# Moving tiles in SBUF: v's tiles and the small ones ahead of the activations' parts, T's second buffer behind its first

## The chip, the core and the metric

The kernel runs on one core of a Trainium2 chip. The metric is the device time of one execution in microseconds (us): 853.65 us before, the median of 3 runs (851.96 to 855.98).

## What is computed

Linear attention over 8 batches, 8 heads, 576 tokens and head size 64, then a feed-forward layer over the 4608 tokens with 512 inputs, 2048 hidden units and 512 outputs:

```python
q_s = softmax(q, axis=-1); k_s = softmax(k, axis=2)     # over the features; over the tokens
kv  = einsum('bhsd,bhse->bhde', k_s, v)
x   = einsum('bhsd,bhde->bhse', q_s, kv)                 # then 4608 x 512
h   = x @ w_in
out = (h * sigmoid(1.702 * h)) @ w_out
```

q, k and v are float32, the two weights are float64.

## The kernel before, in words

**Stages.** The 4608 tokens go in nine blocks t of 512 (TB). For each block the attention part makes x, transposed, in four tiles; the feed-forward part then makes eight steps, each with two of the sixteen groups of 128 hidden units (`pair(t, step)` says which two: ascending in even blocks, descending in odd ones).

**Precision by parts.** Each operand of the feed-forward matmuls is split into a high part and a low part, both float32r; a product is three matmuls (high by high, high by low, low by high) into the same PSUM bank.

**First product of a step.** In blocks 0 and 1 it is `plain1` (line 794): per group and 128 inputs three matmuls with 128x128 weights from wj and 512 columns of xp. In blocks 2 to 8 it is `ffn1` (line 841): a two-by-two product made by seven products instead of eight (a Strassen scheme) over halves of 256 tokens. Each of the seven is six matmuls with 128x128 weights and 256 columns. Four of the seven (products 6, 7, 5, 4 in the code) take their weights from T, sums of weight blocks that block 1 computes once and keeps in DRAM; three (1, 2, 3) take them from wj. The streamed operand is always xo. T has two buffers, `wt(0)` and `wt(1)`, here T0 and T1: a step uses buffer `pair % 2`, so in blocks 2 to 8 (56 steps) 28 steps take T0 and 28 take T1. wj has two buffers likewise (wj0x and wj1x).

**Second product.** `ffn2` (line 904) makes, one step later, eight units (four banks by two groups), each of three matmuls with 128x128 weights from the activations' parts (gh, the high one, and gl, the low one) and 512 streamed columns of w, the parts of w_out: 24 matmuls per step, 72 steps. gh and gl have two buffers, used by `step % 2`: gh0/gl0 and gh1/gl1. So in line 904 the activations are the stationary operand and the weights are streamed; in lines 794 and 841 it is the other way about.

In TensorE's queue the units of the second product lie between the products of the next step. A program at build time (`Plan`) sets the order of all instructions from costs and due times; it looks at no address. The attention work of the next block (lines 582 to 587, 634, 683, 704) lies between the steps as well.

**Where tiles lie.** `sb` makes a tile in one pool with one buffer per tag. Tiles are laid one behind the other in the order in which their tags are first asked for, without holes here; the bytes per partition of a tile are the product of its shape without the first number, times 4. Almost all tiles are a multiple of 512 bytes. The exceptions, which shift all that comes behind them: each of the four vt (2 x 4 x 65 x 4 = 2080 bytes, 32 over a multiple of 512), vl (8 x 65 x 4 = 2080, 32 over), the two qm and r (32 each), and `first` (64). Counted from ident, modulo 512, this gives in the kernel before:

| tile | place modulo 512 |
|---|---|
| gh0, gh1, gl0, gl1 | 0 |
| wj, T0 (in the place of `wide`) | 256 |
| T1 (asked for at its first use, behind w and x tiles) | 320 |
| w, xp, xo | 320 |

Slices inside these tiles start at multiples of 512 bytes, so the distance of a matmul's streamed operand from its stationary one, modulo 512, is 64 for wj and T0 (lines 794 and 841), 0 for T1 (line 841), and 320 for the second product (line 904).

Of the kernel before, what the change touches and what calls it, by code (L numbers as in the profile page):

```python
# [10 lines left out]
F32R = mybir.dt.float32r  # L11
# [125 lines left out]
def efficient_attention_then_gelu_ffn(  # L137
# [28 lines left out]
    B, H, S, D = q.shape  # L166
    NTOK, DM = out.shape
    FF = w_out.shape[0]
    P = 128
    C = 4  # L170
    TB = P * C
    HT = TB // 2
    NB = NTOK // TB
    NP = H // 2
# [4 lines left out]
    CM = SM // P  # L179
    ST = S - SM  # L180
    W = D + 1
# [11 lines left out]
    def sb(name, shape, dtype=F32, tag=None):  # L193
        return const.tile(shape, dtype, name=name, tag=tag or name)

    ident = sb("ident", [P, P])
    kvn = [sb(f"kvn{i}", [P, NP, D]) for i in range(2)]
    gt = [[sb(f"g{i}{u}", [P, 2, HT]) for i in range(2 - u)] for u in range(2)]
    gs = [[sb(f"g{s}{i}", [P, 2, 2, HT], F32R) for i in range(2)] for s in "hl"]
    tt = sb("tt", [P, 4, HT])  # L200
    tmp = [sb(f"tmp{i}", [P, DM]) for i in range(2)]
    kt = [sb(f"kt{i}", [P, 2, CM, D]) for i in range(NP)]
    vt = [sb(f"vt{i}", [P, 2, CM, W]) for i in range(NP)]
    qt = [sb(f"qt{i}", [P, C, 2, D]) for i in range(NP)]
    qT = [sb(f"qT{i}", [P, TB]) for i in range(2)]
    mx = [sb(f"mx{i}", [P, 2, D]) for i in range(NP)]
    m1 = sb("m1", [P, 2, 2, D])
    qm = [sb(f"qm{i}", [P, 2 * C]) for i in range(2)]
    r_ = sb("r", [P, 2, NP])
    rs = [r_[:, i] for i in range(2)]  # L210
    kl, vl = sb("kl", [P, H, D]), sb("vl", [P, H, W])
    wj = [[sb(f"wj{i}{jj}", [P, 2, KC, P], F32R) for jj in range(2)] for i in range(2)]
    wts = {}

    def wt(i):
        if i not in wts:
            wts[i] = sb(f"wt{i}", [P, 2, 4, 2 * P], F32R, tag=f"wt{i}")
        return wts[i]


    wide = sb("wide", [P, 4, DM], tag="wt0")
    kept = [[dram.tile([P, 2 * DM], F32, name=f"kept{p}{jj}") for jj in range(2)] for p in range(NS)]
    kept_t = [dram.tile([P, 4 * DM], F32, name=f"kept_t{p}") for p in range(NS)]

# [779 lines left out]
```

## Time and profile before

| | |
|---|---|
| median of 3 runs | 853.65 us |
| the profiled execution, its own time | 853.69 us |
| its span, first to last instruction | 851.9 us |
| TensorE busy | 843.5 us |
| VectorE, ScalarE, GpSimd busy | 525.6, 487.2, 114.3 us |

The span is 1.8 us shorter than the time of that execution: what lies around the first and last instruction. In the profile PE is TensorE with its matmuls, PEld its weight loads, which overlap the matmuls. Matmuls are pipelined, so the duration of one in a row is longer than the distance from its start to the start of the next; times of a stretch are taken from starts. L841 is line 841 of the kernel. Names like `bank<-xo,wt` are output, then inputs, without buffer numbers: T0 and T1 are both "wt", and are told apart by the time at which they run.

### The profile page before, as it was taken

To read this page: it belongs to the slowest core of one execution; us is meant where nothing else is said; L and a number is where in the kernel's file an instruction comes from. 1 tells how busy PE (TensorE), PEld (TensorE's weight loads), DVE (VectorE), ACT (ScalarE), POOL (GpSimd) and SP (SyncE) were. 2 spreads that over 40 slices of the span, in tenths; PEclk is the share of its full clock that TensorE was granted. 3 is DMA by queue.
4 is the path that set the end of the run, shared out by engine and by line. 5 is a ranking of instruction groups with operands and counts; after the bars stand their busy time and mean duration, and the time that the engine had idled before them with its cause. 6 is when DMAs were issued, how large, how long until landed. Compare 5 with 4: busy or idle time off the path is not lost.

```text
span 851.9 us, 14617 instructions
## 1 busy us (share of the span) xinstructions
PE 843.5 (99%) x5643; PEld 722.3 (85%) x5644; DVE 525.6 (62%) x1082; ACT 487.2 (57%) x833; POOL 114.3 (13%) x175
## 2 busy tenths in 40 slices
PE   9999999999999999999999999999999999999998
PEld 4687787778888898888888998899888899889986
DVE  8899896999627875467554765375356533453333
ACT  5799769768537758465744675464356433343322
POOL 1000020120113011111211121100110011101110
PEclk9999999999999999999999999999999999999999
DMA  9999935893479467564845665623654165416541
GB/s 290 283 339 359 265 132 187 263 320 133 129 233 239 129 161 223 173 186 100 246 158 163 165 184 171 177 88 116 204 162 138 50 198 174 148 50 198 173 148 50
DMA packets 127845, 155.63 MB, mean 183 GB/s; under 512 B 76576, under 2 KB 105760, under 8 KB 121376
## 3 DMA queue, kind: packets, MB, share of 16 engines
q0 software_dynamic: 25248, 83.37, 31.7%
q1 hardware_dynamic: 102528, 71.32, 28.2%
q8 instruction: 45, 0.74, 0.4%
q14 instruction: 24, 0.20, 0.1%
HBM read 128.45 MB, written 26.21 MB: 182 GB/s over the span
## 4 chain that ended last, share of the span: by engine, by line
PE 87%; DVE 6%; DMA 4%; ACT 1%; issue 1%; POOL 0%; SPq 0%; DVEq 0%; ACTq 0%; POOLq 0%
PE bank L904 42%; PE bank L841 33%; PE bank L794 5%; DMA raw<-in_moe_w_out 3%; PE bank L634 2%; PE bank L704 2%; PE bank L683 2%; PE bank L296 1%; DVE w L368 1%; DVE gl L812 1%; DVE wide L333 1%; DVE raw L337 0%; PE bank L582 0%; PE bank L583 0%; DMA vt<-in_v 0%
## 5 line engine op out<-in xcount | busy, mean ns | idle before, releaser
L904 PE MATMUL bank<-w,gh 128*128 128x512 f32 x1152 | 361.0, 395 | 0.0
L904 PE MATMUL bank<-w,gl 128*128 128x512 f32 x576 | 226.3, 393 | 0.4 <-DVE gl L812 0.4
L904 PEld LDWEIGHTS bank<-w,gh 128*128 128x128 f32 x1152 | 192.7, 188 | 25.0 <-issue 2.7
L841 PEld LDWEIGHTS bank<-xo,wt 128*128 128x128 f32 x1344 | 187.8, 188 | 17.8
L841 PE MATMUL bank<-xo,wt 128*128 128x256 f32 x1344 | 193.8, 281 | 0.0
L841 PE MATMUL bank<-xo,wj 128*128 128x256 f32 x1008 | 146.2, 280 | 0.5 <-ACT tt L865 0.5
L841 PEld LDWEIGHTS bank<-xo,wj 128*128 128x128 f32 x1008 | 136.3, 188 | 12.1 <-issue 1.6
L854 DVE TENSOR_TENSOR g<-bank,tt 128x256 f32<-128x256 f32 x168 | 71.0, 423 | 102.9 <-PE bank L841 101.3
L904 PEld LDWEIGHTS bank<-w,gl 128*128 128x128 f32 x576 | 108.3, 188 | 24.9 <-DVE gl L812 0.9
L857 ACT ACTIVATE g<-g 128x512 f32<-128x512 f32 x112 | 58.8, 525 | 121.8 <-DVE g L854 118.8
L854 DVE TENSOR_TENSOR tt<-bank,tt 128x256 f32<-128x256 f32 x112 | 47.3, 423 | 130.3 <-PE bank L841 96.3
L397 POOL DMA_DIRECT2D wj<-kept x96 | 59.4, 619 | 364.1 <-PE bank L841 307.0
L794 PE MATMUL bank<-xp,wj 128*128 128x512 f32 x384 | 103.8, 396 | 1.2 <-ACT g L809 0.9
L885 DVE TENSOR_TENSOR gl<-g,gh 128x512 fp32r<-128x512 f32 x112 | 77.3, 691 | 23.3 <-ACT gh L882 22.7
L794 PEld LDWEIGHTS bank<-xp,wj 128*128 128x128 f32 x384 | 71.2, 188 | 19.6 <-ACT g L809 1.3
L882 ACT CAST gh<-g 128x512 fp32r<-128x512 f32 x112 | 69.5, 621 | 3.5
L545 POOL PARTITION_ALL_REDUCE mx<-mx x32 | 32.3, 1009 | 192.9 <-DVE mx L541 167.4
L857 ACT ACTIVATE g<-bank 128x256 f32<-128x256 f32 x56 | 21.6, 386 | 53.3 <-PE bank L841 52.5
L865 ACT COPY tt<-bank 128x256 f32<-128x256 f32 x56 | 20.8, 372 | 50.6 <-PE bank L841 50.3
L397 POOL DMA_DIRECT2D wt<-kept_t x42 | 22.2, 530 | 148.8 <-PE bank L841 148.8
L687 ACT COPY qT<-bank 128x512 f32<-128x512 f32 x36 | 20.5, 588 | 22.3 <-PE bank L683 21.9
L664 ACT ACT_TABLE_LOAD x25 | 32.1, 1283 | 0.4
(103 smaller groups left out, 802.4 us busy)
## 6 DMA issues: line engine op xcount, KB each, us to landing
wt<-kept_t POOLq DMA_DIRECT2D x42, 1024.0 KB, 5.2
wj<-kept POOLq DMA_DIRECT2D x54, 512.0 KB, 3.7
wj<-kept POOLq DMA_DIRECT2D x42, 256.0 KB, 4.9
out<-tmp SPq DMA_DIRECT2D x36, 256.0 KB, 2.8
kt<-in_k SPq DMA_DIRECT2D x32, 256.0 KB, 4.1
raw<-in_moe_w_in SPq DMA_DIRECT2D x16, 512.0 KB, 8.4
raw<-in_moe_w_out SPq DMA_DIRECT2D x16, 512.0 KB, 7.1
kept<-wj SPq DMA_DIRECT2D x16, 512.0 KB, 6.8
```

The source lines that it names most:

```text
L397: "POOL", 1.0, (key,), (ring,), R(t, step - 2, off), lambda: nc.gpsimd.dma_start(out=out(), in_=src), size=size
L545: nc.gpsimd.partition_all_reduce(flat, flat, P, bass_isa.ReduceOp.max)
L664: nc.scalar.activation(x, x, AF.Exp)
L687: plan.add("ACT", act(TB), (PB,), (Q,), rank, lambda: nc.scalar.copy(qT[hp % 2], pq))
L794: nc.tensor.matmul(bank[bk], w[:, l, c, :], x[:, r], start=c == 0 and e == 0, stop=c == KC - 1 and e == 2)
L841: nc.tensor.matmul(ph[bk], w, x[:, r, c, :], start=opens and c == 0 and e == 0, stop=c == 1 and e == 2, skip_group_check=True,)
L854: return lambda: nc.vector.tensor_tensor(out=o, in0=ph[bk], in1=x, op=ALU.add)
L857: return lambda: nc.scalar.activation(o, x, AF.Gelu_apprx_sigmoid)
L865: vec("ACT", act(n), (ZB,), (A,), 2, lambda: nc.scalar.copy(a, ph[Z]))
L882: vec("ACT", act(2 * n), half, H, slot, lambda c=c, gh=gh: nc.scalar.copy(gh, c))
L885: nc.vector.tensor_tensor(out=gl, in0=c, in1=gh.bitcast(F32), op=ALU.subtract)
L904: nc.tensor.matmul(bank[c], l, r, start=first_ and e == 0, stop=last and e == 2)
```

## The change

Only the order in which the tiles are asked for is changed. vl, qm and r come first, ahead of ident; the second buffers of gh and gl come behind vt, which comes behind their first buffers; T1 is asked for right behind `wide` (T0's place). No instruction, no size and no plan entry changes.

```diff
+    vl = sb("vl", [P, H, W])
+    qm = [sb(f"qm{i}", [P, 2 * C]) for i in range(2)]
+    r_ = sb("r", [P, 2, NP])
+    rs = [r_[:, i] for i in range(2)]
     ident = sb("ident", [P, P])
     kvn = [sb(f"kvn{i}", [P, NP, D]) for i in range(2)]
     gt = [[sb(f"g{i}{u}", [P, 2, HT]) for i in range(2 - u)] for u in range(2)]
-    gs = [[sb(f"g{s}{i}", [P, 2, 2, HT], F32R) for i in range(2)] for s in "hl"]
+    gs = [[sb(f"g{s}0", [P, 2, 2, HT], F32R)] for s in "hl"]
+    vt = [sb(f"vt{i}", [P, 2, CM, W]) for i in range(NP)]
+    for s, g in zip("hl", gs):
+        g.append(sb(f"g{s}1", [P, 2, 2, HT], F32R))
     tt = sb("tt", [P, 4, HT])
     tmp = [sb(f"tmp{i}", [P, DM]) for i in range(2)]
     kt = [sb(f"kt{i}", [P, 2, CM, D]) for i in range(NP)]
-    vt = [sb(f"vt{i}", [P, 2, CM, W]) for i in range(NP)]
...
-    qm = [sb(f"qm{i}", [P, 2 * C]) for i in range(2)]
-    r_ = sb("r", [P, 2, NP])
-    rs = [r_[:, i] for i in range(2)]
-    kl, vl = sb("kl", [P, H, D]), sb("vl", [P, H, W])
+    kl = sb("kl", [P, H, D])
     wj = [[sb(f"wj{i}{jj}", [P, 2, KC, P], F32R) for jj in range(2)] for i in range(2)]
-    wts = {}
+
+    wide = sb("wide", [P, 4, DM], tag="wt0")
+    wts = {1: sb("wt1", [P, 2, 4, 2 * P], F32R)}
...
-    wide = sb("wide", [P, 4, DM], tag="wt0")
```

Counted from the first tile, modulo 512, vl, qm and r take 32 + 64 + 32 = 128, so gh0 and gl0 lie at 128; the four vt add 128, so gh1, gl1, wj, T0 and T1 lie at 256; `first` adds 64, so w, xp and xo lie at 320. The distance, streamed minus stationary, becomes:

| matmuls | before | after |
|---|---|---|
| L794 and L841 with wj, L841 with T0 | 64 | 64 |
| L841 with T1 (28 steps x 24) | 0 | 64 |
| L904 with gh0, gl0 (864) | 320 | 192 |
| L904 with gh1, gl1 (864) | 320 | 64 |

## The prediction

> **What bounds the kernel.** I read first the page with its busy shares and the chain that ended last, then the groups of instructions, then the timeline of TensorE step by step.
>
> ```profile
> span 851.9 us, 14617 instructions
> ...
> PE 843.5 (99%) x5643; PEld 722.3 (85%) x5644; DVE 525.6 (62%) x1082; ACT 487.2 (57%) x833; POOL 114.3 (13%) x175
> ...
> PE 87%; DVE 6%; DMA 4%; ACT 1%; issue 1%; POOL 0%; SPq 0%; DVEq 0%; ACTq 0%; POOLq 0%
> ...
> L904 PE MATMUL bank<-w,gh 128*128 128x512 f32 x1152 | 361.0, 395 | 0.0
> ...
> L841 PE MATMUL bank<-xo,wt 128*128 128x256 f32 x1344 | 193.8, 281 | 0.0
> ...
> L841 PE MATMUL bank<-xo,wj 128*128 128x256 f32 x1008 | 146.2, 280 | 0.5 <-ACT tt L865 0.5
> ```
>
> TensorE is busy for 99% of the span and is 87% of the chain, and the two feed-forward lines have no idle time worth naming before their matmuls (0.0 to 0.5 us per group). So what counts is how fast TensorE goes through a fixed row of matmuls. No instruction changes; time can only come from the distance between starts of neighbouring matmuls, if that depends on where operands lie. Whether it does, the trace of before can show, because its T0 and T1 steps run the same instructions with distances of 64 and 0.
>
> From 768.9 us on, six steps follow each other with no attention work between them. These timeline rows are the first product with T in each step (start, duration, line, operands); the last row is the start of the step behind:
>
> ```profile
> 768.92 0.86 PE L841 MATMUL bank<-xo,wt 128*128 128x256 f32 x6
> ...
> 779.39 0.87 PE L841 MATMUL bank<-xo,wt 128*128 128x256 f32 x6
> ...
> 789.83 0.88 PE L841 MATMUL bank<-xo,wt 128*128 128x256 f32 x6
> ...
> 800.25 0.84 PE L841 MATMUL bank<-xo,wt 128*128 128x256 f32 x6
> ...
> 810.50 0.88 PE L841 MATMUL bank<-xo,wt 128*128 128x256 f32 x6
> ...
> 821.03 0.87 PE L841 MATMUL bank<-xo,wt 128*128 128x256 f32 x6
> ...
> 831.56 0.86 PE L841 MATMUL bank<-xo,wt 128*128 128x256 f32 x6
> ```
>
> Pairs run upward in even blocks, downward in odd ones, and by that the steps from 768.92, 789.83 and 810.50 use T1, those from 779.39, 800.25 and 821.03 use T0. T1 steps last 10.47, 10.42 and 10.53 us, mean 10.473; T0 steps 10.44, 10.25 and 10.53, mean 10.407; all six 62.64 / 6 = 10.44. The view by tile gives the matmuls with T in each of these six steps, in the same order (minimum, median and maximum duration in ns):
>
> ```profile
> L841 PE MATMUL bank<-xo,wt x24: 274/282/287, 768.9 to 776.5; 128*128 128x256 f32 x24
> ...
> L841 PE MATMUL bank<-xo,wt x24: 279/279/281, 779.4 to 786.9; 128*128 128x256 f32 x24
> ...
> L841 PE MATMUL bank<-xo,wt x24: 277/282/287, 789.8 to 797.4; 128*128 128x256 f32 x24
> ...
> L841 PE MATMUL bank<-xo,wt x24: 276/276/276, 800.2 to 807.6; 128*128 128x256 f32 x24
> ...
> L841 PE MATMUL bank<-xo,wt x24: 278/282/287, 810.5 to 818.1; 128*128 128x256 f32 x24
> ...
> L841 PE MATMUL bank<-xo,wt x24: 279/280/283, 821.0 to 828.6; 128*128 128x256 f32 x24
> ```
>
> Each T1 step has matmuls from 274 or 278 up to 287 ns with a median of 282. Each T0 step is nearly uniform, but at 279, 276 or 280. The view by source line gives the second product's matmuls with gh in the three T0 steps:
>
> ```profile
> L904 PE MATMUL bank<-w,gh x16: 392/393/394, 780.8 to 789.4; 128*128 128x512 f32 x16
> ...
> L904 PE MATMUL bank<-w,gh x16: 388/390/392, 801.6 to 810.0; 128*128 128x512 f32 x16
> ...
> L904 PE MATMUL bank<-w,gh x16: 388/397/397, 822.4 to 831.1; 128*128 128x512 f32 x16
> ```
>
> So at one distance there are three rhythms, each held through a whole step: a short one (276 and 390, step 10.25), a middle one (279 and 393, step 10.44), a long one (280 and 397, step 10.53). The rhythms before and behind each T1 step differ: middle before the 789.83 step, short behind it; short before 810.50, long behind it. I read this as a phase between streamed reads and weight loads, which distance 64 keeps and distance 0 disturbs. What sets it otherwise is attention work. The same two views for three T0 steps behind three such stretches, T and gh rows of each:
>
> ```profile
> L841 PE MATMUL bank<-xo,wt x18: 279/280/283, 326.4 to 329.8; 128*128 128x256 f32 x18
> ...
> L904 PE MATMUL bank<-w,gh x16: 388/397/397, 324.4 to 332.3; 128*128 128x512 f32 x16
> ...
> L841 PE MATMUL bank<-xo,wt x18: 279/279/280, 371.8 to 375.2; 128*128 128x256 f32 x18
> ...
> L904 PE MATMUL bank<-w,gh x12: 392/393/394, 371.2 to 377.6; 128*128 128x512 f32 x12
> ...
> L841 PE MATMUL bank<-xo,wt x18: 276/276/276, 475.4 to 478.7; 128*128 128x256 f32 x18
> ...
> L904 PE MATMUL bank<-w,gh x14: 388/390/392, 474.1 to 481.1; 128*128 128x512 f32 x14
> ```
>
> One is long (324 us), one middle (371 us), one short (474 us). So attention leaves any of the three.
>
> **The change part by part.**
>
> *T1 from distance 0 to 64.* 28 steps. If the rhythms stay equally frequent, a T1 step comes to the mean T0 step: 28 x (10.473 - 10.407) = 28 x 0.067 = 1.9 us gained. From the durations alone it would be 24 matmuls x (282 - 278.3) ns x 28 = 2.5 us; I take the steps' own lengths, since the second product between is in them. All of this lies on the path, as TensorE has no gap to put it in. When TensorE is faster by 0.6% in these steps nothing becomes late: VectorE and ScalarE are busy for less than two thirds of the span, and idle 0.5 us per group is all that TensorE waits for them.
>
> *gh and gl from 320 to 192 and 64.* 64 against 320 is shown: in blocks 0 and 1 the first product has 512 columns too, at 64, between units of the second one at 320. Timeline rows from there:
>
> ```profile
> 208.62 0.85 PE L794 MATMUL bank<-xp,wj 128*128 128x512 f32 x3
> 209.31 0.62 PE L904 MATMUL bank<-w,gh 128*128 128x512 f32 x2
> ...
> 210.00 0.85 PE L794 MATMUL bank<-xp,wj 128*128 128x512 f32 x3
> 210.68 0.62 PE L904 MATMUL bank<-w,gh 128*128 128x512 f32 x2
> ```
>
> A unit of three at 64 lasts 209.31 - 208.62 = 0.69 us, one at 320 lasts 210.00 - 209.31 = 0.69, the next at 64 lasts 0.68. So 864 matmuls that go to 64 change by nothing. 192 occurs nowhere among these matmuls. The bounds: like 64, nothing; like 0, what the last matmul of a unit shows when the weights that are loaded beside it are T1's. The view by source line for gl in a T0 step and in the T1 step behind it:
>
> ```profile
> L904 PE MATMUL bank<-w,gl x9: 393/394/394, 800.0 to 810.3; 128*128 128x512 f32 x9
> ...
> L904 PE MATMUL bank<-w,gl x9: 390/392/403, 810.3 to 820.8; 128*128 128x512 f32 x9
> ```
>
> The maximum goes from 394 to 403 and the median not up at all. By the T rows distance 0 costs 282 - 279 = 3 ns; by this maximum 9 ns. 864 x 3 to 9 ns = 2.6 to 7.8 us lost is the far end; at the other end 192 could bring the short rhythm to the 28 steps that use gh0, 28 x (10.44 - 10.25) = 5.3 us gained. I take nothing, as 64 and 320, on both sides of 192, agree to 0.01 us per unit.
>
> *The attention matmuls.* The starts of vt's and kt's tiles move from 0, 32, 64 and 96 apart to 384 to 480, vl's and kl's from 0 to 256. The timeline rows of one block's four pairs of heads, with the row behind them:
>
> ```profile
> 470.05 0.69 PE L634 MATMUL bank<-vt,kt 128*64 128x65 f32 x16
> ...
> 470.69 0.64 PE L634 MATMUL bank<-vt,kt 128*64 128x65 f32 x16
> ...
> 471.27 0.64 PE L634 MATMUL bank<-vt,kt 128*64 128x65 f32 x16
> ...
> 471.86 0.64 PE L634 MATMUL bank<-vt,kt 128*64 128x65 f32 x16
> ...
> 472.54 0.62 PE L841 MATMUL bank<-xo,wj 128*128 128x256 f32 x3
> ```
>
> They take 0.64, 0.58, 0.59 and 0.68 us, the first and last with a change of shape at the edge; the two inner ones, 32 and 64 apart, agree to 0.01. 32 pairs x 0 to 0.06 us is 0 to 1.9 us either way; I take 0, by the inner rows. The other tiles that move are operands of VectorE, ScalarE and transfers, with the same sizes and the same order; they cost nothing while TensorE is the bound.
>
> *The sum.* Against the profiled execution, 853.69 us (span 851.9 and 1.8 around it; the median of three is 853.65, the same): 853.69 - 1.9 = 851.8 us. With it goes an uncertainty which the kernel before has less of. Its T1 steps turn the rhythm over; afterwards one lasts until attention work, and a few stretches weigh more. All 56 steps short: 56 x (10.44 - 10.25) = 10.6 us gained, 843.1. All long: 56 x (10.53 - 10.44) = 5.0 us lost, 858.7.
>
> **The rivals.** *The short rhythm is kept.* With all distances at odd multiples of 64 the phase might settle into the short rhythm and survive attention work. For it: through the T0 step at 800 us it holds to the nanosecond (276 / 276 / 276). Against it: middle and long hold as well, and three stretches left three rhythms. Price: up to 10.6 us, 843.1; it decides from 4.3 us of gain, 849.4, on, that is with about half of the steps short and the others evenly split between 10.44 and 10.53 (0.52 x 10.25 + 0.48 x 10.485 = 10.36).
>
> *192 behaves like 0.* Place: the units with gh0 and gl0, half of line 904. Then every second step carries matmuls 3 to 9 ns longer, 2.6 to 7.8 us, against the 1.9 gained: 854.4 to 859.6, so slower than before. It decides when the cost is over 2.2 ns per matmul. For it: 320 and 64 leave the same remainder modulo 256, and 192 does not, so their agreement need not reach to it. Against it: 192 is as far from 0 as 320 is.
>
> *Nothing changes.* T1 also differs from T0 in its absolute place and data; if that, and not the distance, makes the 282 ns, the T1 steps stay as they are: 853.7. Against it: the different rows with T0 show that the same instruction with the same tile changes by 4 ns, so something about timing between reads is at work, not data. The Trainium skill ("SBUF — State Buffer", section "Who interferes with whom") gives TensorE two independent read ports, one for the streamed operand and one for weight loads, and says that it never waits on anyone; by that rule the operands' places would not matter and the time would be this rival's 853.7, and the T1 rows of this trace speak against it.
>
> **How the numbers follow.** A measurement of this kernel tells about 0.5% from no change: faster is below 849.4, slower above 857.9. My forecast (T1 like T0, rhythms mixed as now) has 0.56; with a spread of about 2 us for the mix, 0.06 of it lie below 849.4 and 0.03 above 857.9. The short rhythm kept has 0.22, all of it faster. 192 like 0 has 0.12, half of it slower. Nothing changes has 0.10. Faster: 0.22 + 0.06 = 0.28. Slower: 0.03 + 0.06 = 0.09. Same: 0.63. The range leaves out the lower half of that case (0.11) and the upper tails (0.09): 846 to 857.5. The time predicted is the forecast's, 851.8; its own range, with half of the attention's 1.9 us and the mix's 2 us, is 849 to 855.
>
> **What would show it.** Right: in steps with T1 the matmuls with T become uniform, at 276, 279 or 280 with a maximum within 4 ns of it, and no step without attention work changes its rhythm; line 904 keeps 390, 393 or 397 for both buffers; the steps' mean is 10.38 to 10.44. The short rhythm kept would show as 276 and 390 in more than half of the steps, behind most attention stretches too. 192 like 0 would show as spread-out durations, to 400 and more, in the steps that use gh0, and rhythms that change there. Nothing changed would be 282 with a maximum of 287 in T1 steps as now. The forecast is wrong above all if the share of the rhythms shifts, for which I have a few stretches as evidence, or if 192 isn't like 64.

## The result, and the profile after

The changed kernel takes 858.61 us (856.67 to 860.07) beside 853.51 us for the kernel before, measured together: a ratio of 1.0056 [1.0045, 1.0066]. It is slower by 5.1 us, 0.6%, where 851.8 us was forecast, and 1.1 us above the range. The profiled execution took 858.71 us, its span is 856.9 us, 5.0 us more than before.

The page of the changed kernel (all lines of code stand five further down: L909 was L904, L846 was L841, L799 was L794):

```profile
span 856.9 us, 14618 instructions
...
PE 848.1 (99%) x5644; PEld 723.7 (84%) x5644; DVE 525.9 (61%) x1082; ACT 488.1 (57%) x833; POOL 114.5 (13%) x175
...
PE 92%; DMA 4%; DVE 2%; ACT 1%; issue 0%; DVEq 0%; SPq 0%
...
L909 PE MATMUL bank<-w,gh 128*128 128x512 f32 x1152 | 363.1, 396 | 0.0
...
L846 PE MATMUL bank<-xo,wt 128*128 128x256 f32 x1344 | 194.1, 281 | 0.0
```

The bound is the same. TensorE is busy for 99% of the span, has no idle time ahead of the feed-forward lines, and its busy time grew by 4.6 us (848.1 against 843.5), nearly all of the 5.0. So the time went where the prediction looked for it, into the distance between the starts of neighbouring matmuls. The page shows it only as 396 ns instead of 395; the steps show more. The timeline of the changed kernel, first product with T of each of the six steps without attention work (start, duration):

```profile
773.43 0.87 PE L846 MATMUL bank<-xo,wt 128*128 128x256 f32 x6
...
783.95 0.87 PE L846 MATMUL bank<-xo,wt 128*128 128x256 f32 x6
...
794.47 0.87 PE L846 MATMUL bank<-xo,wt 128*128 128x256 f32 x6
...
804.99 0.87 PE L846 MATMUL bank<-xo,wt 128*128 128x256 f32 x6
...
815.51 0.87 PE L846 MATMUL bank<-xo,wt 128*128 128x256 f32 x6
...
826.03 0.87 PE L846 MATMUL bank<-xo,wt 128*128 128x256 f32 x6
```

The step behind them starts at 836.55. Each of the six lasts 10.52 us. Before they lasted 10.47, 10.44, 10.42, 10.25, 10.53 and 10.53, mean 10.44. The view by tile for the first three of them, T rows and gh rows (minimum, median and maximum duration in ns, then first and last start):

```profile
L846 PE MATMUL bank<-xo,wt x24: 279/280/284, 773.4 to 781.0; 128*128 128x256 f32 x24
...
L909 PE MATMUL bank<-w,gh x17: 388/397/398, 773.0 to 783.5; 128*128 128x512 f32 x17
...
L846 PE MATMUL bank<-xo,wt x24: 279/280/283, 783.9 to 791.6; 128*128 128x256 f32 x24
...
L909 PE MATMUL bank<-w,gh x17: 388/397/397, 783.5 to 794.0; 128*128 128x512 f32 x17
...
L846 PE MATMUL bank<-xo,wt x24: 279/280/284, 794.5 to 802.1; 128*128 128x256 f32 x24
...
L909 PE MATMUL bank<-w,gh x17: 388/398/398, 794.0 to 804.5; 128*128 128x512 f32 x17
```

T1 and T0 steps now look alike, as predicted: T1's maximum is 284 where it was 287. But they look alike in the long rhythm (280 and 397). The short one (276 and 390) and the middle one do not appear, and the steps from 783.95, which have T0 and gh1 at 64 as before, are as long as those with gh0 at 192.

How 192 does that can be seen where a step with gh1 hands over to one with gh0. The timeline of the changed kernel between two attention stretches (starts are to be subtracted; a unit of the second product is two matmuls with gh and one with gl):

```profile
347.59 0.84 PE L846 MATMUL bank<-xo,wj 128*128 128x256 f32 x6
348.27 0.62 PE L909 MATMUL bank<-w,gh 128*128 128x512 f32 x2
...
348.97 0.63 PE L909 MATMUL bank<-w,gh 128*128 128x512 f32 x2
...
349.66 0.87 PE L846 MATMUL bank<-xo,wj 128*128 128x256 f32 x6
350.37 0.63 PE L909 MATMUL bank<-w,gh 128*128 128x512 f32 x2
...
351.07 0.87 PE L846 MATMUL bank<-xo,wt 128*128 128x256 f32 x6
```

Up to 348.27 the step before runs in the short rhythm: its last unit of six lasts 348.27 - 347.59 = 0.68 us. Then come the first two units with gh0, of 0.70 and 0.69 us, and the next unit of six, with the same weights' place as ever, lasts 350.37 - 349.66 = 0.71. One pair of units at 192 has turned the short rhythm into the long one, and it stays. It is the only place in this trace where the short rhythm meets gh0 undisturbed: the two other short passages run into attention work.

Over the whole run, T's rows give the first and last start of a matmul with T, so nearly the length of blocks 2 to 8. Before:

```profile
L841 PE MATMUL bank<-xo,wt x1344: 274/280/388, 216.9 to 839.1; 128*128 128x256 f32 x192
```

After:

```profile
L846 PE MATMUL bank<-xo,wt x1344: 276/280/384, 218.8 to 844.2; 128*128 128x256 f32 x192
```

839.1 - 216.9 = 622.2 us became 844.2 - 218.8 = 625.4, 3.2 more. Worked out from the starts of all units with no other work beside them: a unit of the second product in these blocks takes 695.0 ns in the mean, 691.1 before, and one of the first product 706.5, 702.9 before. 452 x 3.9 + 392 x 3.6 ns = 3.2 us. In blocks 0 and 1 it is 693.9 for 687.3 and, with plain1, 693.0 for 687.1: 124 x 6.6 + 128 x 5.9 ns = 1.6 us. Together that reckons 4.8 of the 5.0 us out of starts of matmuls that are next to each other. It takes the mean of the undisturbed units for all of them. In blocks 2 to 8 it meets the 3.2 us of T's rows. In blocks 0 and 1 it is less sure: the first matmul with T starts 1.9 us later, but that stretch also holds a wait near 40 us, behind a transfer of w_out, that left TensorE idle for 2.28 us here and for 0.90 before.

### The profile page after: what moved, and what is told of

The parts are those of the page before. It is cut to its first block, busy times and chain, and to the rows that moved or that the text cites. A ratio compares the mean times of both kernels' runs of the same rounds, so it can differ in the third digit from the quotient of the medians.

```text
span 856.9 us, 14618 instructions
## 1 busy us (share of the span) xinstructions
PE 848.1 (99%) x5644; PEld 723.7 (84%) x5644; DVE 525.9 (61%) x1082; ACT 488.1 (57%) x833; POOL 114.5 (13%) x175
## 4 chain that ended last, share of the span: by engine, by line
PE 92%; DMA 4%; DVE 2%; ACT 1%; issue 0%; DVEq 0%; SPq 0%
PE bank L909 44%; PE bank L846 33%; PE bank L799 7%; PE bank L639 2%; PE bank L709 2%; DMA kept<-wj 2%; PE bank L688 2%; DMA raw<-in_moe_w_out 1%; PE bank L301 1%; DMA qt<-in_q 1%; PE bank L587 0%; PE bank L588 0%; DVE wj L373 0%; DVE kt L561 0%; DMA out<-tmp 0%
## 5 line engine op out<-in xcount | busy, mean ns | idle before, releaser
L909 PE MATMUL bank<-w,gh 128*128 128x512 f32 x1152 | 363.1, 396 | 0.0
L909 PE MATMUL bank<-w,gl 128*128 128x512 f32 x576 | 226.4, 393 | 0.0
L909 PEld LDWEIGHTS bank<-w,gh 128*128 128x128 f32 x1152 | 192.9, 188 | 26.1 <-issue 2.7
L846 PEld LDWEIGHTS bank<-xo,wt 128*128 128x128 f32 x1344 | 187.9, 188 | 18.1
L846 PE MATMUL bank<-xo,wt 128*128 128x256 f32 x1344 | 194.1, 281 | 0.0
L846 PE MATMUL bank<-xo,wj 128*128 128x256 f32 x1008 | 147.4, 281 | 0.5 <-ACT tt L870 0.5
L846 PEld LDWEIGHTS bank<-xo,wj 128*128 128x128 f32 x1008 | 137.1, 188 | 12.2 <-issue 1.6
L909 PEld LDWEIGHTS bank<-w,gl 128*128 128x128 f32 x576 | 108.4, 188 | 24.8
L799 PE MATMUL bank<-xp,wj 128*128 128x512 f32 x384 | 104.8, 398 | 2.3 <-ACT g L814 2.3
L799 PEld LDWEIGHTS bank<-xp,wj 128*128 128x128 f32 x384 | 71.1, 188 | 21.8 <-ACT g L814 2.7
```

What stands on the lines that cost most here:

```text
L799: nc.tensor.matmul(bank[bk], w[:, l, c, :], x[:, r], start=c == 0 and e == 0, stop=c == KC - 1 and e == 2)
L846: nc.tensor.matmul(ph[bk], w, x[:, r, c, :], start=opens and c == 0 and e == 0, stop=c == 1 and e == 2, skip_group_check=True,)
L909: nc.tensor.matmul(bank[c], l, r, start=first_ and e == 0, stop=last and e == 2)
```

## The experiments

The theory behind the first four, A: 192 is a bad distance for the 512-column matmuls of the second product, and it ends the short rhythm. B: no distance is bad, but two buffers at different distances disturb the rhythm. C: T1 at 0 used to turn the rhythm over, and without that the kernel stays in whichever rhythm it falls into, mostly the long one; then moving T1 alone costs the time. The four lay T1 and the parts of g out in the other combinations. The kernel before took 853.12 us beside them.

**T1 alone.** The kernel before, with T1 asked for behind T0; only T1's distance changes (0 to 64):

```diff
-    wts = {}
+    wide = sb("wide", [P, 4, DM], tag="wt0")
+    wts = {1: sb("wt1", [P, 2, 4, 2 * P], F32R)}
...
-    wide = sb("wide", [P, 4, DM], tag="wt0")
```

> The kernel before with T1 alone moved behind T0: T1's products at distance 64, the second product at 320 with both buffers. Theory A (distance 192 makes the units of gh0 and gl0 longer and ends the short rhythm; T1 at 64 is a small gain): T1 steps hold their rhythm, all units of the second product at 687 or 698 ns, 851.0 to 852.5 us against 853.5 before. Theory B (it is not 192 but that the two buffers lie at different distances): the same, 851.0 to 852.5. Theory C (products at distance 0 turned the rhythm over and so shared the short one out; without them the long one stays): 855 to 858.

848.28 us, ratio 0.9935 [0.9921, 0.9949]: 4.8 us faster, and below the range that A and B gave. C, by which moving T1 is what costs the time, falls. The view by tile for T in the last stretch without attention work, in the kernel before and, in the second fence, with T1 alone moved:

```profile
L841 PE MATMUL bank<-xo,wt x174: 274/280/287, 765.4 to 839.1; 128*128 128x256 f32 x174
```

```profile
L841 PE MATMUL bank<-xo,wt x168: 276/276/276, 764.9 to 833.8; 128*128 128x256 f32 x168
```

All 168 matmuls last 276 ns. The short rhythm, once there, holds through seven steps. Over the whole run the median of T's matmuls is 276 too, and blocks 2 to 8 take 616.7 us:

```profile
L841 PE MATMUL bank<-xo,wt x1344: 276/276/392, 217.1 to 833.8; 128*128 128x256 f32 x192
```

**All at 64.** The changed kernel with vt ahead of the first buffers too, so that gh0 and gl0 go from 192 to 64:

```diff
-    gs = [[sb(f"g{s}0", [P, 2, 2, HT], F32R)] for s in "hl"]
     vt = [sb(f"vt{i}", [P, 2, CM, W]) for i in range(NP)]
+    gs = [[sb(f"g{s}0", [P, 2, 2, HT], F32R)] for s in "hl"]
```

> The kernel after with vt ahead of both buffers of gh and gl: every matmul of the feed-forward part at distance 64. Theory A: no unit of the second product at 693 to 703 in place of 687, 851.0 to 852.5 us. Theory B: one distance for both buffers, so the same, 851.0 to 852.5. Theory C: as after, 857 to 859, since T1 is at 64 here too.

850.58 us, ratio 0.9958 [0.9943, 0.9973]. Taking 192 out of the changed kernel makes it about 8 us faster (0.9958 for 1.0056), and faster than the kernel before; this too is just below the range of A and B.

**The parts of g alone.** The changed kernel with T1 where it was, at distance 0:

```diff
-    wide = sb("wide", [P, 4, DM], tag="wt0")
-    wts = {1: sb("wt1", [P, 2, 4, 2 * P], F32R)}
+    wts = {}
...
+    wide = sb("wide", [P, 4, DM], tag="wt0")
```

> The kernel after with T1 asked for at its first use, as before: T1's products at distance 0 again, the second product at 192 with gh0, gl0 and 64 with gh1, gl1. Theory A: as after, and without T1's gain of about 1 to 2 us, 859.0 to 860.5 us. Theory B: the same. Theory C: distance 0 turns the rhythm over again, 853 to 855.

858.34 us, ratio 1.0056 [1.004, 1.0071], a little under what A gave; C's 853 to 855 falls once more. The move of g's parts costs 5.2 us by itself, all that the whole change costs: beside it, T1 at 0 or at 64 makes no difference (1.0056 both times).

**Both buffers at 192.** The changed kernel with vt behind the second buffers:

```diff
-    vt = [sb(f"vt{i}", [P, 2, CM, W]) for i in range(NP)]
     for s, g in zip("hl", gs):
         g.append(sb(f"g{s}1", [P, 2, 2, HT], F32R))
+    vt = [sb(f"vt{i}", [P, 2, CM, W]) for i in range(NP)]
```

> The kernel after with vt behind both buffers of gh and gl: the second product at 192 with both, T1 at 64. Theory A: the cost of 192 comes twice, units of gh1 at 693 to 703 as well, 860.5 to 863 us. Theory B: one distance for both, 851.0 to 852.5. Theory C: as after, 857 to 859.

859.77 us, ratio 1.0078 [1.0059, 1.0096]. Equal buffers are no cure, so B falls. A has the direction, with less time than it gave: twice the units at 192 cost only some 2 us more than the changed kernel (1.0078 for 1.0056), so most of what 192 takes is taken by the first half of the units. From the starts, a unit of three that follows another of its kind in blocks 2 to 8 takes 696.2 ns with gh0 and 687.0 with gh1 in the changed kernel; 696.2 and 697.1 here; 686.7 for both with all at 64; 688.0 and 687.0 in the kernel before. So 192 costs 3 ns per matmul in such a unit, in the changed kernel 56 units x 9 ns = 0.5 us in these blocks, and the rest of its price there goes with the short rhythm: in the profiled execution of each kernel, units of the first product that last at most 684 ns are 80 of 349 before, 12 after, none with both buffers at 192, 224 with T1 alone moved, 178 with all at 64 (349 to 351 undisturbed units in each).

**The distance by itself.** A kernel with only series of matmuls, 36 with 512 columns or 48 with 256, each with its own weight load and the streamed operand at one of sixteen distances, each series three times with other matmuls ahead:

```python
def weights(i):
    return st[:, i % 4 * P : (i % 4 + 1) * P]
def stream(d, n, i):
    return mv[:, d // 4 + i % 3 * 1024 : d // 4 + i % 3 * 1024 + n]
```

> Computes none of the reference: series of float32r matmuls alone, each with its own weight load, 36 with 512 columns or 48 with 256, at one distance per series (0 to 480 in steps of 32, modulo 512, streamed minus stationary), each series three times behind other matmuls that shift its phase; zeros or sums of them go out. Theory A (the distance itself sets the pace): with 512 columns 229 ns from start to start at 64 and at 320, and 232 or more at 192 and 0; with 256 columns 113 or 118 at 64 and 320, and more than 118 at 0. Where A's cycle is 256 bytes, d and d + 256 agree; where it is 512, 448 need not be as 192 is. Rival D (no distance is long by itself, only the change from units of 256 columns to units of 512 is): all series of one width agree within 1 ns.

The timeline of that kernel, one series each at 0, 64, 128, 192, 256, 320 and 384 (start, duration of all 36):

```profile
486.13 8.39 PE L42 MATMUL bank<-mv,st 128*128 128x512 f32 x36
...
503.34 8.50 PE L46 MATMUL bank<-mv,st 128*128 128x512 f32 x36
...
520.73 8.55 PE L50 MATMUL bank<-mv,st 128*128 128x512 f32 x36
...
538.15 8.62 PE L54 MATMUL bank<-mv,st 128*128 128x512 f32 x36
...
555.68 8.35 PE L58 MATMUL bank<-mv,st 128*128 128x512 f32 x36
...
572.89 8.45 PE L62 MATMUL bank<-mv,st 128*128 128x512 f32 x36
...
590.16 8.61 PE L66 MATMUL bank<-mv,st 128*128 128x512 f32 x36
```

0 and 256 are the shortest, 64 and 320 next, 128, 192 and 384 the longest. By the starts in the steady part of the series, one matmul takes 227 ns at 0 and at 256 (without the first series of the kernel, 244 ns at 0), 228.9 at 64 and at 320, 233.3 at 192 and at 448, 232.4 to 232.7 at 128 and 384: a distance and the same plus 256 agree within 0.3 ns in all eight pairs of the sixteen distances. 192 costs 4.4 ns more than 64 in a series of its own. A had this for 192, but not for 0, for which it gave 232 or more. D, by which all series of one width agree, falls. With 256 columns one distance can have two paces. The same series at 64, first and second time:

```profile
167.33 5.65 PE L47 MATMUL bank<-mv,st 128*128 128x256 f32 x48
...
401.88 5.88 PE L47 MATMUL bank<-mv,st 128*128 128x256 f32 x48
```

That is 113.3 and 117.8 ns per matmul; 192, 320 and 448 show the same two, while 0 and 256 have only 120. Six of them make 680 or 707 ns, as the kernel's units of 0.68 and 0.71 us: two rhythms with nothing but matmuls. The first two series at 64 differ in nothing but what ran ahead, so that decides.

**Pairs of units.** Alternating units as in a step, six matmuls of 256 columns at one distance and three of 512 at another, all 64 combinations of multiples of 64, three times:

```python
for u in range(6):
    for i in range(6):
        first[x](4 + u % 2, i)
    for i in range(3):
        second[g](u % 4, i)
```

> Computes none of the reference: six times a unit of six matmuls with 256 columns and a unit of three with 512, as the feed-forward steps have them, for each of the 64 pairs of distances (first unit, second unit) of 0 to 448 in steps of 64, each three times from other phases. Theory A: with 64 for the first unit and 64 or 320 for the second a series can hold 680 + 687 = 1367 ns per pair of units; with 192 for the second none does, and it takes 1394 to 1410; with 0 for the first none does either. Rival D: 1367 occurs with any pair of distances, by the phase at the start alone.

At (320, 320) both rhythms occurred. The timeline of that kernel, a short and a long passage:

```profile
414.40 0.87 PE L53 MATMUL bank<-mv,st 128*128 128x256 f32 x6
415.11 0.86 PE L54 MATMUL bank<-mv,st 128*128 128x512 f32 x3
415.80 0.87 PE L53 MATMUL bank<-mv,st 128*128 128x256 f32 x6
...
974.31 0.84 PE L53 MATMUL bank<-mv,st 128*128 128x256 f32 x6
974.99 0.85 PE L54 MATMUL bank<-mv,st 128*128 128x512 f32 x3
975.68 0.84 PE L53 MATMUL bank<-mv,st 128*128 128x256 f32 x6
```

A pair takes 1.40 us in the first and 1.37 in the second. In the mean, 1367 ns appeared in one of the three series at (320, 320) and nowhere with a 192 or a 0 in it, as expected; (64, 192), the changed kernel's pair, took 1400 in all three. That is no more than the long rhythm at (64, 64), 1406 in all three: what 192 takes away is the short one. In the kernel above the streamed operand was moved and the stationary one stayed; here it is the other way about, and the period of 256 bytes shows again ((192, 64) and (448, 320) take 1380, (0, 0) and (256, 256) 1406), so the distance counts, not the place of one operand. That only one series of twelve with 64 and 320 found the short rhythm leaves open how often a kernel finds it. A new thing was (192, 64): 1380 in all three series, whatever ran ahead.

**First product at 192, second at 64.** If 1380 from any start held in the kernel, it would need no luck. For that wj, T0 and T1 go to 192, g's parts to 64 (wj and T's places ahead of vt, gs behind it):

```diff
-    gs = [[sb(f"g{s}0", [P, 2, 2, HT], F32R)] for s in "hl"]
-    vt = [sb(f"vt{i}", [P, 2, CM, W]) for i in range(NP)]
-    for s, g in zip("hl", gs):
-        g.append(sb(f"g{s}1", [P, 2, 2, HT], F32R))
...
     wts = {1: sb("wt1", [P, 2, 4, 2 * P], F32R)}
+    vt = [sb(f"vt{i}", [P, 2, CM, W]) for i in range(NP)]
+    gs = [[sb(f"g{s}{i}", [P, 2, 2, HT], F32R) for i in range(2)] for s in "hl"]
```

> All tiles as after, laid out so that T and wj are at 192 from xo and xp, and gh, gl at 64 from w. Theory A (a unit's pace follows from the two distances modulo 256, as in the run of pairs, where 192 for the first unit and 64 for the second gave 692 + 688 = 1380 ns from any phase): no short, middle and long rhythm any more, first products at 692 behind every attention stretch, a step of 7 x 1380 + 687 = 10.35 us, 56 x (10.44 - 10.35) = 5 us less than before; in blocks 0 and 1 the first product at 192 costs up to 384 x 4.4 ns = 1.7 us; 848 to 851 us. Rival E (units of the same kind in a row and attention work break the pattern of the run of pairs): mixed unit times, 852 to 856. Theory of the change's name (64 and 192 are alike): 851 to 853.

852.08 us, ratio 0.9983 [0.9973, 0.9992], where the kernel before took 853.65: A's 848 to 851 is missed, and the time lies in E's range. The pair is there, as the timeline of this kernel shows (start to start 1.38 us):

```profile
782.59 0.85 PE L843 MATMUL bank<-xo,wt 128*128 128x256 f32 x6
...
783.97 0.85 PE L843 MATMUL bank<-xo,wt 128*128 128x256 f32 x6
```

But in blocks 0 and 1 the first product has 512 columns, and there its undisturbed units take 696 ns for 687 before. And a long rhythm is left: 101 of 350 undisturbed units of the first product take 700 ns and more, through whole steps behind some attention stretches.

**T alone at 192.** The same with wj moved behind vt, to 64:

```diff
-    wj = [[sb(f"wj{i}{jj}", [P, 2, KC, P], F32R) for jj in range(2)] for i in range(2)]
...
     vt = [sb(f"vt{i}", [P, 2, CM, W]) for i in range(NP)]
+    wj = [[sb(f"wj{i}{jj}", [P, 2, KC, P], F32R) for jj in range(2)] for i in range(2)]
     gs = [[sb(f"g{s}{i}", [P, 2, 2, HT], F32R) for i in range(2)] for s in "hl"]
```

> The same with T alone at 192; wj, gh and gl at 64. Theory A: four of seven first products at 692 and the steps between them by the phase in which these leave TensorE; no cost in blocks 0 and 1, since wj is at 64; 847 to 850 us. Rival E: three rhythms as with all at 64, 849 to 852.

849.84 us, ratio 0.9952 [0.9939, 0.9964]. With no 512-column matmul of the feed-forward part at 192 the kernel is 2.2 us faster than the one above. The time lies in the ranges of both A and E; by the units E is nearer, as they are mixed (112 of 349 at most 684 ns, 159 at 685 to 699, 78 at 700 and more).

**First product at 192, second at 256.** The kernel before with only qm ahead of ident, then kl, gs, vl and r behind the attention tiles, T1 behind T0, and vt last of all:

```diff
+    qm = [sb(f"qm{i}", [P, 2 * C]) for i in range(2)]
     ident = sb("ident", [P, P])
...
+    kl = sb("kl", [P, H, D])
+    gs = [[sb(f"g{s}{i}", [P, 2, 2, HT], F32R) for i in range(2)] for s in "hl"]
+    vl = sb("vl", [P, H, W])
...
```

> T and wj at 192, gh and gl at 256, which is 0 modulo 256. Theory A: 680 + 700 = 1380 ns per pair of units, from any phase; units of the second product in a row at 227 ns per matmul; 847 to 850 us, though 0 was the long distance for T1 in the kernel before. Rival E: 852 to 856. A theory that 0 is long for any operand: over 858.

853.95 us, ratio 1.0009 [0.9997, 1.002]: A is missed, and E's range holds it. The second product's units, short in their own series at 256, take 699 ns behind a unit of the first product here, which A had from the pairs. What A had wrong is the rest: units of the first product take 680 ns from the fourth of a step on, where both kinds alternate (197 of 350 in all), but 706 to 707 in the first three of most steps, around the places where two of a kind stand next to each other; and units of the second product in a row take 687 to 689 ns, not 3 x 227 = 681. A good distance for one line alone isn't a good one beside another.

**What sets apart 848.3 and 850.6.** T1 alone was faster than all at 64. The two kernels differ in g's distance (320 or 64) and in the places of the attention's tiles. Two kernels change one of these each in the kernel with T1 alone moved, and that kernel was taken again, all beside 853.03 us for the kernel before. Gs ahead of wj, g at 64:

```diff
-    gs = [[sb(f"g{s}{i}", [P, 2, 2, HT], F32R) for i in range(2)] for s in "hl"]
...
     kl, vl = sb("kl", [P, H, D]), sb("vl", [P, H, W])
+    gs = [[sb(f"g{s}{i}", [P, 2, 2, HT], F32R) for i in range(2)] for s in "hl"]
```

> e1 with gh and gl asked for right ahead of wj: the second product at 64 in place of 320, no attention tile moved against another. Theory F (64 and 320 are one distance; what sets e2 apart from e1 is the moved attention tiles): 848.3 us within 1. Rival H (320 is better than 64): 850.6 within 1, as e2.

849.27 us, ratio 0.9947 [0.9927, 0.9967]. The attention's tiles moved as in the change, g left at 320 (both buffers ahead of vl, qm and r):

```diff
+    gs = [[sb(f"g{s}{i}", [P, 2, 2, HT], F32R) for i in range(2)] for s in "hl"]
+    vl = sb("vl", [P, H, W])
+    qm = [sb(f"qm{i}", [P, 2 * C]) for i in range(2)]
+    r_ = sb("r", [P, 2, NP])
...
+    vt = [sb(f"vt{i}", [P, 2, CM, W]) for i in range(NP)]
...
```

> The second product at 320 and the first at 64, as e1, with vl, qm and r ahead of ident and vt ahead of tt, so that the attention tiles lie to each other as in after and e2. Theory F: 850.6 us within 1, as e2. Rival H: 848.3 within 1, as e1.

849.71 us, ratio 0.9955 [0.9939, 0.9972]. And T1 alone once more, unchanged:

> e1 once more, beside the other two. If the share of the short rhythm belongs to the layout: 847.3 to 849.3 us, and short in 55 to 70% of the first-product units again. If it is chance of the one occasion: anywhere from 848 to 853.

849.50 us, ratio 0.995 [0.9931, 0.9969]. The three can't be told apart, and the second look at T1 alone is 1.2 us above the first. The first two fall into F's ranges and outside H's, but by a few tenths, and the third lies between them, 0.2 us above the range for its layout; short units are 210, 214 and 204 of some 350, 58 to 61%. So neither g at 64 instead of 320 nor the places of the attention's tiles has a price that shows, and the 2.3 us between T1 alone and all at 64 are put down to scatter. A part of that scatter is the granted clock: with all at 64 the four executions at a clock of 1.0 took 848.03 to 850.56 us, the four at 0.997 to 0.998 took 850.60 to 851.72, and T1 alone had none below 0.999 the first time. T1 alone moved, 0.9935 and 0.995, beats both kernels; no version here is clearly better, and those with every feed-forward distance at 64 or 320, or T at 192, can't be told from it.

## Why the prediction was wrong

**The step that failed** is "gh and gl from 320 to 192 and 64", where it says of 192: "I take nothing, as 64 and 320, on both sides of 192, agree to 0.01 us per unit". Moving g's parts alone costs 5.2 us, and taking 192 out of the changed kernel gives about 8 back. 64 and 320 agree because they are the same distance: the paces repeat every 256 bytes in the series kernel. So they say nothing about 192. The prediction had this in the rival's "For it" (the same remainder modulo 256) and set "192 is as far from 0 as 320 is" against it. That is so, and doesn't help: modulo 256 both are 64 away from the nearest multiple, but on opposite sides, and the side matters (228.9 at 64, 233.3 at 192).

**The rival "192 behaves like 0"** had the place, and its bounds (854.4 to 859.6) hold the time, but by luck, as the way is another. In a series, 0 is the fastest distance for 512 columns and 192 among the slowest. Nor did durations spread to 400 and more: gh's stay at or below 398 in the steps shown. The own cost at 192 is 3 ns per matmul in units that follow one of their kind; the larger part comes by the rhythm, in steps with gh1 too.

**T1 from 0 to 64** was right in its sign and its sight (uniform durations, no turning over), and its term was too small for T1 alone: 1.9 us predicted, 4.8 and 3.5 measured. What failed is its condition, that the rhythms stay equally frequent. T1 steps had thrown the kernel out of the short rhythm again and again. Without them it lasts from one attention stretch to the next: 224 and, in the second look, 204 of some 350 undisturbed units, against 80. That is the rival "the short rhythm is kept", which came true in the half of the change that has no 192: its deciding point, about half of the steps short and 849.4 us, is about what T1 alone moved reached. In the whole change it couldn't show, as beside 192 the short rhythm doesn't last. So the two parts don't add: -4.8 and +5.2 alone, +5.1 together, and in the whole change T1's move is worth nothing.

**"Nothing changes"** fell: moving T1 alone changed the time. The Trainium skill ("SBUF — State Buffer", section "Who interferes with whom") gives TensorE two independent read ports and says that it never waits on anyone. By that rule, the prediction says, the operands' places would not matter. The series kernel disagrees: 227 to 234 ns per matmul of 512 columns by the distance alone.

**Right**: 64 for 320 costs nothing (849.27 and 849.71 beside 849.50), the attention's tiles cost nothing that shows, TensorE stayed the bound.

**Open.** Which rhythm an attention stretch leaves behind is not explained; in the kernels without 192 and 0 the short units went from 178 to 224, and with the same kernel, T1 alone, they were 224 and 204. Why 256 bytes is the period, and by what the units at 192 end the short rhythm, isn't shown either. Nor is the start of a run: the first matmul with T starts at 216.9 us before, 217.1 with T1 alone and 219.2 with all at 64, though no feed-forward matmul of blocks 0 and 1 lies at 192 in any of these. A part is the wait near 40 us behind the transfer of w_out, 0.90 us before and 3.52 with all at 64; why that transfer lands at different times isn't shown.

## What to carry to other kernels

When a kernel is a fixed row of matmuls, the place of its operands can be worth half a per cent either way, as here; look at starts, not at mean durations, and at neighbours of the moved operand, since the cost can lie in steps that it isn't part of. Before reading "A and B agree, so what lies between them does too", test whether A and B are the same case: a short kernel of series over all distances shows the period and the order for little. And make one move at a time: here the half that helped was hidden behind the half that hurt.

## What the hardware showed that was not expected

- The pace of float32r matmuls, each with its own weight load, depends on the distance of streamed and stationary operand in a partition modulo 256 bytes: 227 ns at 0 to 234.4 at 160 for 512 columns, in series of such matmuls alone.
- At 256 columns one and the same series at 64 runs at 113.3 or 117.8 ns per matmul for its whole length, by what ran ahead; at 0 only at 120.
- The best distance depends on the neighbours: 0 is the fastest for 512 columns in a series, and T1 at 0 disturbs the kernel; 256 columns at 192 beside 512 columns at 64 hold 1380 ns per pair from every start, the reverse pair takes 1400.
